# One input load moved from SyncE's queue to GpSimd's, and five filler matmuls fewer, at the start of an attention-plus-MLP kernel

## The chip, the cores and the metric

The kernel runs on one core of a Trainium2 chip. The metric is the device time of one execution in microseconds (us); for the kernel before it is the median of six runs. Five engines work side by side, each through its own list of instructions in order: TensorE (PE, matrix products), VectorE (DVE), ScalarE (ACT), GpSimd (POOL) and SyncE (SP, which here only issues DMAs). DMAs are issued from the lists of SP and GpSimd (one tiny one from ACT) and are carried out by 16 DMA engines; an engine that needs the data waits on a semaphore until the whole transfer has landed.

## The reference

Four batches, eight heads, 768 positions, head dimension 64. A linear attention with a decay `lam` per head is followed by a two-layer MLP with a gated activation. All inputs and the output are float32.

```
for each block b of 64 positions:
    intra = ((q_b k_b^T) * Dmask) v_b          # Dmask[i, j] = lam^(i-j) for i >= j, else 0
    inter = (q_b * lam^(i+1)) kv_state
    out_b = intra + inter
    kv_state = lam^64 * kv_state + (k_b * lam^(63-j))^T v_b
x = out, heads side by side                     # 3072 tokens x 512
h = x @ w_in                                    # 512 -> 2048
y = (h * sigmoid(1.702 h)) @ w_out              # 2048 -> 512
```

## The kernel before

The 768 positions are cut into waves. Waves 0 and 1 (`ND = 2`) each take two of the four batches with 256 positions of each; the four later waves take 128 positions of all four batches. So each wave gives 512 tokens to the MLP. A wave's attention is done while TensorE still works on the MLP of the wave before; only wave 0 has nothing ahead of it. The order of the instructions is written out by hand (`tc.manual_schedule()`, L457): wave 0 line by line (L458 to L512), then a list of MLP steps (`main`) into which attention steps (`side`) are put at given places (L545 to L577). The engines carry out their lists in just that order.

**Loads.** `load(0)` (L104) issues k, q, v of batch 0 and then k, q, v of batch 1 of wave 0 through SP, each 512 KB, most of them in two halves of four heads; v of batch 1 is one transfer. Each contiguous piece is 512 bytes. The weights are float32 in memory and bf16 in SBUF, so they are loaded by DMAs that convert, from GpSimd's list: `load_w_in(0)` to `(4)` (L175, tiles of 256, 256, 512, 512, 512 columns) and `load_w_out(0)` to `(3)` (L180). `gate_pool` (L451) makes GpSimd wait for the first half of v of batch 0 before it issues the first weights. `gate_sync` (L454, used at L506) makes SP wait until `w_out1` has landed; only then does SP issue `load(1)`, the inputs of wave 1.

**Attention of wave 0.** `do_cast` (L189) multiplies k or q by powers of `lam` and writes bf16: on VectorE for batch 0 and for q of batch 1, on GpSimd for k of batch 1 (L480). `turn_pe` (L228) transposes the result on TensorE and copies it out of PSUM with VectorE or ScalarE. `cast_v` (L219) converts v to bf16; of batch 1, one half on ScalarE and one on GpSimd (L499). `d_scores` (L247) makes the scores, VectorE masks them (L263); `split=True` lets ScalarE copy half of the scores out of PSUM first (L261). `d_one`/`d_state` (L280, L269) make the state from k and v, `d_out` (L304) the output from scores and v.

**The MLP.** `mlp1` (L387) and, for wave 0's first columns, `mlp1_half` (L397) compute the first layer from the `w_in` tiles; `mlp2` (L411) the second from `w_out`. In wave 0 the halves use `w_in0` and `w_in1`; the first full step of L393 is the first to use `w_in2`.

**Order around the change.** GpSimd's list at this place: gate on v of batch 0, `load_w_in(0)`, four multiplications of k of batch 1 (L198), `load_w_in(1)`, `load_w_in(2)`, its half of v of batch 1 (L211), `load_w_in(3)`, `(4)`, `load_w_out(0)` to `(3)`. TensorE's list: `fill(n)` (L139) puts n matmuls on a zero tile in front of or between the first transposes and scores; their result is never read. On TensorE, `mlp1_half(0, 0, 0)` (L509) stands ahead of `d_one(0, 1)` (L510), the first matmuls to read v of batch 1. On ScalarE, the half of v of batch 1 stands between the two copies of batch 1's scores.

Of the kernel before, what the change touches and what calls it, by code (L numbers as in the profile page):

```python
# [24 lines left out]
def kernel(  # L25
# [13 lines left out]
    nc = tc.nc  # L39
# [36 lines left out]
    def load_one(w, c, nm, src):  # L76
        x = ld.tile([P, H, 2 * D], f32, tag=f"{nm}{c}", name=f"{nm}f")
        if w < ND:
            n = H if w or (nm == "v" and c) else H // 2
            for h in range(0, H, n):  # L80
                nc.sync.dma_start(  # L81
                    out=x[:, h : h + n],
                    in_=src[2 * w + c, h : h + n, 0 : 2 * P, :].rearrange("h (s a) d -> s h (a d)", a=2))
        else:
            nc.sync.dma_start(out=x.rearrange("p h (a d) -> p (h a) d", a=2),
                              in_=src[2 * c : 2 * c + 2, :, w * P : (w + 1) * P, :].rearrange("b h s d -> s (b h) d"))
        loaded[w, c, nm] = x

    def load(w, nms="kqv"):
        src = {"k": k, "q": q, "v": v}  # L90
        if w < ND:
            for c in range(HF):
                for nm in nms:
                    load_one(w, c, nm, src[nm])
        else:
            for nm in nms:
                for c in range(HF):
                    load_one(w, c, nm, src[nm])
# [3 lines left out]
    ones = const.tile([1, P], f32)  # L102
    nc.vector.memset(ones, 1.0)
    load(0)  # L104

    nc.scalar.preload_act_table_set("natural_log_exp_and_others")
# [29 lines left out]
    def acc(name, dt=f32, shape=None, tag="a"):  # L136
        return ps.tile(shape or [P, 4, P], dt, tag=tag, bufs={"a": 5, "mm": 3}[tag], name=name)

    def fill(n, new=None):  # L139
        if new:  # L140
            fill_ps[0] = acc("ps_fill", shape=[P, W], tag=new)
        for _ in range(n):
            nc.tensor.matmul(fill_ps[0], zero[:, 0:P], zero, start=True, stop=True)  # L143
# [31 lines left out]
    def load_w_in(j):  # L175
        c0 = sum(IN_CH[:j]) * P
        nc.gpsimd.dma_start(  # L177
            out=w_in_sb[j], in_=moe_w_in.rearrange("(kc ki) f -> ki kc f", ki=P)[:, :, c0 : c0 + IN_CH[j] * P])
# [10 lines left out]
    def do_cast(w, c, nm, eng, g=None):  # L189
        if g in (None, 0):  # L190
            cast[w, c, nm] = work.tile([P, 2, HD], bf16, tag=f"{nm}s{c}", name=f"{nm}s")
        f, x = loaded[w, c, nm], cast[w, c, nm]
        if w < ND:
            pw = {"k": kd_pow, "q": qd_pow}[nm]
            for R in (0, 1) if g is None else (g,):
                for j in range(2):
                    h = slice(4 * R + 2 * j, 4 * R + 2 * j + 2)
                    eng.tensor_tensor(x.rearrange("p a (r i j d) -> p r j i a d", i=2, j=2, d=D)[:, R, j],  # L198
                                      f[:, h].rearrange("p i (a d) -> p i a d", a=2),
                                      pw[:, h].unsqueeze(3).to_broadcast([P, 2, 2, D]), op=MUL)  # L200
        else:
            pw = {"k": k_pow, "q": q_pow}[nm]
            n = 2 * H // 4
            for j in range(2):
                eng.tensor_tensor(x.rearrange("p b (r i j d) -> p j (b r) i d", i=2, j=2, d=D)[:, j],  # L205
                                  f.rearrange("p h (a d) -> p (h a) d", a=2).rearrange("p (n j i) d -> p j n i d", j=2, i=2)[:, j],
                                  pw.rearrange("p b (r j i) -> p j (b r) i", i=2, j=2)[:, j].unsqueeze(3).to_broadcast([P, n, 2, D]),
                                  op=MUL)
# [19 lines left out]
    def turn_pe(w, c, nm, copy=act_copy, g=None):  # L228
        x = cast[w, c, nm]
        rr = list(range(NP)) if g is None else [2 * g, 2 * g + 1]  # L230
        t = acc("ps_t", bf16, [P, len(rr), 2, P])
        for i, r in enumerate(rr):
            for a in range(2):
                nc.tensor.transpose(t[:, i, a, :], x[:, a, r * P : (r + 1) * P], ident)  # L234
        if g in (None, 0):
            trans[w, c, nm] = work.tile([P, 2 * NP, P], bf16, tag=f"{nm}T{c}", name=f"{nm}T")
        copy(trans[w, c, nm][:, 2 * rr[0] : 2 * rr[0] + 2 * len(rr)], t.rearrange("p r a s -> p (r a) s"))
# [9 lines left out]
    def d_scores(w, c, pp, split=False):  # L247
        kT = trans[w, c, "k"]
        s2 = [acc("ps_s") for _ in range(2)]
        for i in range(2):  # L250
            r = 2 * pp + i
            for a in range(2):
                for blk, bs in enumerate((A, Z)):
                    for h, hs in enumerate((A, Z)):
                        nc.tensor.matmul(s2[h][bs, 2 * i + a, :], kT[hs, 2 * r + a, bs], q_of(w, c, hs, r, blk),  # L255
                                         start=True, stop=True)
        for h in range(2):
            sm = work.tile([P, 2, 2, P], bf16, tag="sm", bufs=8, name="sm")
            flat = s2[h].rearrange("p (i a) s -> p i (a s)", i=2)
            if split and h:  # L260
                nc.scalar.copy(sm.rearrange("p i a s -> p i (a s)"), flat)  # L261
                flat = sm.rearrange("p i a s -> p i (a s)")
            nc.vector.tensor_tensor(sm.rearrange("p i a s -> p i (a s)"), flat,  # L263
                                    mask_d.rearrange("p o a b s -> p o (a b s)").to_broadcast([P, 2, 2 * P]), op=MUL)
            masked[w, c, pp, h] = sm
# [185 lines left out]
    def gate_pool(x):  # L451
        nc.gpsimd.tensor_copy(behind_q, x)
# [4 lines left out]
    with tc.manual_schedule():  # L457
# [4 lines left out]
            nc.scalar.activation(blk_pow[rows].rearrange("p (r i) -> p r i", i=2),  # L462
                                 ln_lam[rows].rearrange("p (r j i) -> p r j i", i=2, j=2)[:, :, j, :], EXP, scale=1.0 * P)
        nc.scalar.activation(warm, q_pow[:, 0, 0:1], GELU)
        fill(5)
        for nm, copies in (("k", (dve_copy, act_copy)), ("q", (act_copy, dve_copy))):
            for g in range(2):
                do_cast(0, 0, nm, nc.vector, g)
            for g in range(2):
                turn_pe(0, 0, nm, copies[g], g)  # L470
                fill(2 if nm == "k" or g == 0 else 0)
        gate_pool(loaded[0, 0, "v"][0:1, 0, 0:1])
        load_w_in(0)
        cast_v(0, 0, (act_copy, act_copy))
        d_scores(0, 0, 0)
        fill(1)
        d_scores(0, 0, 1)
        fill(3)
        for g in range(2):
            do_cast(0, 1, "k", nc.gpsimd, g)  # L480
        for j in (1, 2):
            load_w_in(j)
        d_one(0, 0, "mm")
# [18 lines left out]
        for j in range(NCH):  # L502
            load_w_out(j)
        nc.gpsimd.affine_select(mask, mask, pattern=[[0, 1], [1, P]], channel_multiplier=-1, base=0,
                                compare_op=mybir.AluOpType.is_ge, fill=0.0)
        gate_sync(w_out_sb[1][0:1, 0, 0:2])  # L506
        load(1)
        d_scores(0, 1, 1, True)
        mlp1_half(0, 0, 0)  # L509
# [36 lines left out]
        for w in range(NW):  # L546
            n = len(main)
            main += mlp_items(w)
            e = len(main)
            x = w + 1  # L550
            if x < ND:
                for c, (k_at, q_at, v_at, k_turn, q_turn, s_at, e_at) in enumerate(
                        ((19, 20, 19, 24, 25.5, 27, 30), (26.5, 28, 28, 29, 30, 32, 34))):
                    side += [(n + k_at, (do_cast, x, c, "k", (nc.vector, nc.gpsimd)[c])),
                             (n + q_at, (do_cast, x, c, "q", nc.vector)),
                             (n + v_at, (cast_v, x, c, ((pool_copy, pool_copy), (act_copy, act_copy))[c])),
                             (n + k_turn, (turn_pe, x, c, "k", act_copy)),
                             (n + q_turn, (turn_pe, x, c, "q", act_copy)),
                             (n + s_at, (start, x, c)), (n + e_at, (end, x, c))]
            elif x < NW:  # L560
                for c in range(HF):
                    tk, tq = (n + 2.1 + 2 * c, n + 4 + c) if x == ND else (n + 4 + 2 * c, n + 5 + 2 * c)
                    side += [(tk, (do_cast, x, c, "k", nc.vector)), (tk, (turn_dma, x, c, "k")),
                             (tq, (do_cast, x, c, "q", nc.vector)), (tq, (turn_dma, x, c, "q")),
                             (n + 10 + 2 * c, (cast_v, x, c, (dve_copy,)))]
                if x == ND:
                    side += [(n + 7, (stores,))]
                t = n + 16
                side += [(t, (n_two, x, 0)), (t + 4, (n_two, x, 1)), (t + 9, (n_rest, x))]
            if w + 2 < NW:  # L570
                side += [(n + (12 if w else 20), (load, w + 2))]
# [36 lines left out]
```

## Time and profile before

| What | Value |
|---|---|
| median of six runs | 208.05 us (207.48 to 208.66) |
| the profiled execution, its own time | 208.51 us |
| the profiled execution, span from first to last instruction | 206.8 us |
| TensorE busy | 201.3 us, 97% of the span |
| VectorE, ScalarE, GpSimd busy | 89.2, 86.1, 16.2 us |
| HBM read, written | 27.26 MB, 6.29 MB |
| filler matmuls (L143) | 20, 8.0 us busy, 518 ns mean |

The span is what the profile's clock runs over; the execution's own time holds 1.7 us more around it. Times in the profile count from the start of the span. A row such as `7.92 0.95 POOL L177 ...` gives start, duration, engine and line; what stands in square brackets is how long the engine had been idle and what released it. A queue marked POOLq or SPq belongs to the engine that issues the DMA. TensorE's busy share says little here: matmuls are pipelined, and fillers count as busy.

### The profile page before, as it was taken

The numbers are of one execution on the slowest core, as the hardware profiler recorded it, in microseconds if no ns is written. First come the engines' busy times: TensorE is split into PE (matmuls) and PEld (weight loads), VectorE is DVE, ScalarE is ACT, GpSimd is POOL, SyncE is SP. The second block draws the span as 40 slices with busy tenths as digits, with TensorE's granted clock in tenths as the row PEclk, the third lists the DMA queues.
The fourth block names the chain that finished last, engine by engine and source line by source line (L and its number), as shares of the span: only waits on it lengthen the run. The fifth ranks groups of instructions, "written<-read, shape, count | busy, mean of one in ns | idle before, by whom it ended". The sixth has DMA issues, their size and how long they took to land.

```text
span 206.8 us, 4295 instructions
## 1 busy us (share of the span) xinstructions
PE 201.3 (97%) x1830; PEld 105.1 (51%) x1830; DVE 89.2 (43%) x160; ACT 86.1 (42%) x158; POOL 16.2 (8%) x37
## 2 busy tenths in 40 slices
PE   7999899999999999999999999999999999999994
PEld 2576344466864464444464444464444454444453
DVE  1793000586961843931743841743841731100121
ACT  4877562147665030566021566021466021565000
POOL 4496000060000000000000000000000000000000
DMA  5999999999997999879971379961360011100112
GB/s 155 335 226 185 201 204 242 270 310 240 249 221 169 214 264 247 200 177 251 236 206 51 103 179 267 222 199 52 101 155 0 36 68 51 51 0 0 54 51 101
DMA packets 87640, 33.82 MB, mean 164 GB/s; under 512 B 67398, under 2 KB 84678, under 8 KB 87622
## 3 DMA queue, kind: packets, MB, share of 16 engines
q1 hardware_dynamic: 82868, 29.37, 56.3%
q0 software_dynamic: 4752, 4.19, 12.9%
q8 instruction: 14, 0.23, 0.5%
q14 instruction: 4, 0.03, 0.1%
q10 hardware_dynamic: 2, 0.00, 0.0%
HBM read 27.26 MB, written 6.29 MB: 162 GB/s over the span
## 4 chain that ended last, share of the span: by engine, by line
PE 88%; DMA 7%; SPq 1%; POOL 1%; issue 0%; DVE 0%; POOLq 0%
PE ps_out L417 41%; PE ps_h L393 35%; DMA w_in<-in_moe_w_in_dram 4%; PE ps_h L405 3%; DMA kf<-in_k_dram 2%; PE ps_s L331 2%; PE ps_o L381 2%; SPq L81 1%; POOL ks L198 1%; PE ps_o L368 1%; PE ps_t L234 1%; PE ps_kv L355 1%; PE ps_o L312 1%; PE ps_s L255 1%; PE ps_kv L275 0%; POOL w_in L177 0%
## 5 line engine op out<-in xcount | busy, mean ns | idle before, releaser
L417 PE MATMUL ps_out<-w_out,g_sb 128*128 128x512 bf16 (+2 forms) x416 | 86.2, 363 | 0.0
L393 PE MATMUL ps_h<-xT,w_in 128*128 128x512 bf16 x336 | 73.5, 379 | 0.8 <-DMA w_in<-in_moe_w_in_dram 0.8
L395 ACT ACTIVATE g_sb<-ps_h 128x512 bf16<-128x512 f32 x84 | 50.2, 597 | 46.1 <-PE ps_h L393 46.1
L417 PEld LDWEIGHTS <-g_sb 128*128 128x128 bf16 x416 | 38.2, 98 | 41.0
L393 PEld LDWEIGHTS <-w_in 128*128 128x128 bf16 x336 | 32.8, 98 | 40.3 <-DMA w_in<-in_moe_w_in_dram 1.1
L421 DVE COPY o_sb<-ps_out 128x512 f32<-128x512 f32 (+2 forms) x26 | 16.9, 650 | 52.4 <-PE ps_out L417 52.4
L339 DVE SCALAR_TENSOR_TENSOR sm<-ps_s,inv_pow,mask 128x512 bf16<-128x512 f32 x32 | 21.8, 742 | 28.5 <-PE ps_s L331 22.3
L385 ACT CAST xT<-ps_o 128x512 bf16<-128x512 f32 x16 | 8.2, 599 | 37.8 <-PE ps_o L381 37.8
L198 DVE TENSOR_TENSOR ks<-kf,kd_pow 128x256 bf16<-128x256 f32 x8 | 2.9, 420 | 22.9 <-DMA kf<-in_k_dram 19.6
L405 PE MATMUL ps_h<-xT,w_in 128*128 128x256 bf16 x96 | 11.4, 273 | 0.0
L205 DVE TENSOR_TENSOR qs<-qf,q_pow 128x512 bf16<-128x512 f32 x16 | 10.3, 683 | 0.0
L205 DVE TENSOR_TENSOR ks<-kf,k_pow 128x512 bf16<-128x512 f32 x16 | 10.3, 683 | 0.0
L405 PEld LDWEIGHTS <-w_in 128*128 128x128 bf16 x96 | 9.0, 98 | 1.6 <-DVE xT L214 0.2
L143 PE MATMUL ps_fill<-zero 128*128 128x512 bf16 x20 | 8.0, 518 | 1.4 <-DVE zero L113 1.4
L263 DVE TENSOR_TENSOR sm<-ps_s,mask_d 128x512 bf16<-128x512 f32 x14 | 8.8, 684 | 0.8 <-PE ps_s L255 0.5
L407 ACT ACTIVATE g_sb<-ps_h 128x512 bf16<-128x512 f32 x12 | 7.2, 598 | 4.3 <-PE ps_h L405 4.3
L359 DVE SCALAR_TENSOR_TENSOR kv<-kv,blk_pow,ps_kv 128x256 bf16<-128x256 bf16 x12 | 5.0, 475 | 6.0 <-PE ps_kv L355 6.0
L217 ACT COPY kT<-ps_t 128x512 bf16<-128x512 bf16 (+1 forms) x4 | 3.2, 797 | 8.1 <-PE ps_t L234 8.1
L198 DVE TENSOR_TENSOR qs<-qf,qd_pow 128x256 bf16<-128x256 f32 x16 | 5.7, 417 | 0.1
L331 PEld LDWEIGHTS <-kT 64*128 64x128 bf16 x128 | 3.6, 94 | 3.4 <-issue 3.4
L214 DVE CAST v_sb<-vf 128x1024 bf16<-128x1024 f32 x8 | 5.1, 683 | 0.0
L331 PE MATMUL ps_s<-qT,kT 64*128 64x128 bf16 x128 | 5.0, 217 | 0.0
(68 smaller groups left out, 91.4 us busy)
## 6 DMA issues: line engine op xcount, KB each, us to landing
vf<-in_v_dram SPq DMA_DIRECT2D x11, 512.0 KB, 6.4
kf<-in_k_dram SPq DMA_DIRECT2D x10, 512.0 KB, 5.8
qf<-in_q_dram SPq DMA_DIRECT2D x10, 512.0 KB, 6.5
out_dram<-o_sb SPq DMA_DIRECT2D x15, 256.0 KB, 2.0
out_dram<-o_sb SPq DMA_DIRECT2D x17, 128.0 KB, 2.4
w_out<-in_moe_w_out_dram POOLq DMA_DIRECT2D x4, 512.0 KB, 16.2
w_in<-in_moe_w_in_dram POOLq DMA_DIRECT2D x3, 512.0 KB, 9.8
kf<-in_k_dram SPq DMA_DIRECT2D x4, 256.0 KB, 3.1
```

The source lines that it names most:

```text
L143: nc.tensor.matmul(fill_ps[0], zero[:, 0:P], zero, start=True, stop=True)
L198: eng.tensor_tensor(x.rearrange("p a (r i j d) -> p r j i a d", i=2, j=2, d=D)[:, R, j], f[:, h].rearrange("p i (a d) -> p i a d", a=2), p ...
L205: eng.tensor_tensor(x.rearrange("p b (r i j d) -> p j (b r) i d", i=2, j=2, d=D)[:, j], f.rearrange("p h (a d) -> p (h a) d", a=2).rearran ...
L263: nc.vector.tensor_tensor(sm.rearrange("p i a s -> p i (a s)"), flat, mask_d.rearrange("p o a b s -> p o (a b s)").to_broadcast([P, 2, 2 * ...
L331: nc.tensor.matmul(s2[h][:, b, :], kT[hs, (b % 2) * NP + p, :], qT[hs, (b % 2) * NP + p, :], start=True, stop=True)
L339: nc.vector.scalar_tensor_tensor(sm, s, inv_pow[:, n : n + 1], mask.to_broadcast([P, B, P]), op0=MUL, op1=MUL)
L385: nc.scalar.copy(xT[w][:, p, :], ps_o.rearrange("p b s -> p (b s)"))
L393: nc.tensor.matmul(h, w_in_sb[j][:, kc, i * P : (i + 1) * P], xT[w][:, kc, :], start=(kc == 0), stop=(kc == KC - 1))
L395: nc.scalar.activation(g_of[w][:, fc, :], h, GELU)
L405: nc.tensor.matmul(h[:, u, :], w_in_sb[j][:, kc, i * P : (i + 1) * P], xT[w][:, kc, cols], start=(kc == 0), stop=(kc == KC - 1))
L417: nc.tensor.matmul(ps_out, g_of[w][:, fc, g * P : (g + 1) * P], w_out_sb[j][:, fc % CW, c0:c1], start=(fc == 0), stop=(fc == FFC - 1))
L421: nc.vector.tensor_copy(o, ps_out)
```

## The change

Two things are done. First, v of batch 1 of wave 0 is left out of `load(0)` and is issued from GpSimd's list after the four multiplications of k of batch 1 and ahead of `load_w_in(1)`. The transfer is the same one: 512 KB, float32 on both sides, into the same tile. Second, the fillers become fewer: 3 in place of 5 after the powers, then 2, 1, 1, 0 in place of 2, 2, 2, 0 behind batch 0's four transposes, and none in place of 1 between its two groups of scores. The four at the very start, the three after the scores and the one further on stay. One line is added at L94, so in the kernel after every later line has a number higher by one, but for those between the filler taken out at L476 and the added load (L477 to L480), which keep theirs.

```diff
         if w < ND:
             n = H if w or (nm == "v" and c) else H // 2
             for h in range(0, H, n):
-                nc.sync.dma_start(
+                (nc.gpsimd if w == 0 and c and nm == "v" else nc.sync).dma_start(
                     out=x[:, h : h + n],
                     in_=src[2 * w + c, h : h + n, 0 : 2 * P, :].rearrange("h (s a) d -> s h (a d)", a=2))
...
             for c in range(HF):
                 for nm in nms:
-                    load_one(w, c, nm, src[nm])
+                    if w or c == 0 or nm != "v":
+                        load_one(w, c, nm, src[nm])
...
         nc.scalar.activation(warm, q_pow[:, 0, 0:1], GELU)
-        fill(5)
+        fill(3)
         for nm, copies in (("k", (dve_copy, act_copy)), ("q", (act_copy, dve_copy))):
             for g in range(2):
                 do_cast(0, 0, nm, nc.vector, g)
             for g in range(2):
                 turn_pe(0, 0, nm, copies[g], g)
-                fill(2 if nm == "k" or g == 0 else 0)
+                fill(2 - g if nm == "k" else 1 - g)
         gate_pool(loaded[0, 0, "v"][0:1, 0, 0:1])
         load_w_in(0)
         cast_v(0, 0, (act_copy, act_copy))
         d_scores(0, 0, 0)
-        fill(1)
         d_scores(0, 0, 1)
         fill(3)
         for g in range(2):
             do_cast(0, 1, "k", nc.gpsimd, g)
+        load_one(0, 1, "v", v)
         for j in (1, 2):
             load_w_in(j)
```

## The prediction, made before the result was known

> **What bounds the kernel now.** I read the chain that ended last first. From 21.40 us on it is TensorE without a gap to the end, so all that counts is when that dense stretch starts and whether it is interrupted. Columns: start us, duration us, what.
>
> ```profile
> 9.35 2.33 POOL ks L198 x4
> 11.68 0.75 POOL w_in L177
> 12.43 8.92 DMA w_in<-in_moe_w_in_dram
> 21.35 0.05 issue
> 21.40 10.53 PE ps_h L393 x48
> ```
>
> The dense stretch starts when `w_in2` has landed, at 21.35. The timeline of the first 22 us shows the work around it.
>
> ```profile
> 7.92 0.95 POOL L177 DMA_DIRECT2D w_in<-in_moe_w_in_dram  x1
> ...
> 11.63 1.55 POOL L177 DMA_DIRECT2D w_in<-in_moe_w_in_dram  x2
> ...
> 13.50 0.61 POOL L211 CAST v_sb<-vf 128x512 bf16<-128x512 f32 x1 [0.32 <-DMA vf<-in_v_dram]
> ...
> 14.73 1.05 PE L405 MATMUL ps_h<-xT,w_in 128*128 128x256 bf16 x8
> ...
> 14.99 0.62 ACT L217 CAST v_sb<-vf 128x512 bf16<-128x512 f32 x1
> ...
> 15.71 0.37 PE L275 MATMUL ps_kv<-v_sb,ks 64*64 64x64 bf16 x12
> ...
> 21.40 0.82 PE L393 MATMUL ps_h<-xT,w_in 128*128 128x512 bf16 x3 [0.81 <-DMA w_in<-in_moe_w_in_dram]
> ```
>
> TensorE was done with all before L393 at 21.40 - 0.81 = 20.59 and stood still 0.81 us for `w_in2`. v of batch 1 landed at 13.48 (7.88 issue + 5.6 to landing, by the issues), 1.5 us before ScalarE got to its half at 14.99; TensorE's L275 at 15.71 follows on that half (done 15.61). Then the DMA by window, three windows: 10.0 to 10.5, 12.5 to 13.0, 20.0 to 21.4 us. Columns: queue, packets, MB, share of 16 engines' time.
>
> ```profile
> q1 hardware_dynamic: 336, 0.17, 113.2%
> ```
> ```profile
> q0 software_dynamic: 159, 0.08, 118.6%
> q1 hardware_dynamic: 49, 0.02, 21.8%
> ```
> ```profile
> q0 software_dynamic: 280, 0.27, 119.1%
> q8 instruction: 1, 0.02, 4.3%
> ```
>
> The 16 engines are full throughout (shares over 100% are overlapping packets), first with SP's loads, then with GpSimd's. The weights were issued at 7.92, yet between 8 and 12 us only 25 software packets start against 2617 hardware ones: GpSimd's transfers run when SP's are through. In the third window one instruction fetch of 4.3% x 16 x 1.4 us = 0.96 us sits on a DMA engine just before `w_in2` lands. Last, the timeline of wave 1's first transposes:
>
> ```profile
> 38.18 1.43 DVE L198 TENSOR_TENSOR ks<-kf,kd_pow 128x256 bf16<-128x256 f32 x4 [19.56 <-DMA kf<-in_k_dram]
> 39.54 0.61 PE L234 MATMUL ps_t<-ident,ks 128*128 128x128 bf16 x8
> ```
>
> VectorE waits 19.56 us for k of wave 1, which lands at about 38.16; its four products end at 39.61, and the second four transposes, which read the later two, run from about 39.54 + 4 x 0.056 = 39.76. So this landing has about 0.1 us of slack. It too hangs on the DMA queue: SP issues it only when `w_out1`, seventh in GpSimd's line of weights, has landed. The start of the kernel is bound by the DMA in two places, at 21.4 and at 39.6.
>
> [...] fillers start 0.42 us apart until 7.4 us and 0.22 us after.
>
> **The change part by part.**
>
> *Fillers.* Removed are two ahead of 5.83, at 0.42 us each, one behind the second and one behind the third transpose (0.2 to 0.4 us each), one at 9.37 (0.22). What waits on the first two: the first transposes start at 5.83, while VectorE's first products were ready at 5.35 + 0.1; so 0.4 us is won. VectorE's kT copy follows (6.50 becomes 6.1, as its products end at 6.06), and everything of batch 0 moves with it: scores 9.02 to about 8.5, masks 9.55 to 9.05, `d_out` and batch 1's q likewise. GpSimd's k of batch 1 does not move, it starts on a landing (9.35), but the transposes on it have room (first pair ready 10.5). The one at 9.37 costs nothing today: the second scores at 9.69 wait on the qT copy, 9.04 + 0.42. Sum: TensorE reaches L405 at 14.2 in place of 14.73. Unknown is the clock: [...] turns, scores and three fillers take about 0.4 + 0.7 + 0.6 us more at half speed, partly beside VectorE's masks. Bounds 0 to 0.6 us lost; I take 0.
>
> *SP's queue without v.* 512 KB in 512-byte packets are 1024 packets. The hardware queue moves 336 in 0.5 us, so its end comes 1024/672 = 1.5 us earlier, at 10.0 to 11.5 by engine in place of 11.5 to 13.0. `w_in0` (512 packets, 32 per engine, at 47 ns apiece: 85 per 0.25 us between 13.25 and 14.5) is then through at 11.5 to 13.0 and lands at about 13 in place of 14.5 (7.92 + 6.6). L405, moved to 14.2, so finds its weights; with `w_in0` at 14.5 it would not have.
>
> *v on GpSimd's queue.* It can be issued only after the four products of k, at 11.65. One issue of L177 takes 0.75 us, with half as many packets; so 0.75 to 1.5 us. [...] Data: 64 packets per engine at 24 ns (the hardware queue's rate, low end) to 47 ns (`w_in0`'s, which read 1 KB each, high end), 1.5 to 3.0 us; I take 28 ns, from the line through 47 ns for 1 KB and 82 ns for 2 KB read (855 packets in 4.4 us), 1.8 us. With 0.4 us to land: 14.8 to 15.3 on undisturbed engines; on the one that fetches instructions (0.96 us at 14.04, then inside this transfer) up to 16.2. Bounds 14.5 to 16.5, taken 15.8.
>
> *Who waits for that.* ScalarE would reach its half at 14.5 and stands until 15.8; behind it are the second copy of scores, the GELU of L405, both state copies, xT. TensorE stands at L275, GpSimd at L211. The whole tail from 14.99 to 20.59 moves by 15.8 - 14.99 = 0.8 us: TensorE is ready for L393 at 21.4. The 0.5 us of the fillers and the 0.81 us of idle time are both eaten; alone this gives no change. Behind L211 in GpSimd's list stand `w_in3` to `w_out3`: issued from about 16.4 in place of 14.05, while the line still has `w_in2` to move until 18 or later; no gap.
>
> *The DMA line.* Bytes are the same, so nothing is gained. Two things are lost. Between `w_in0` (through at 11.5 to 13.0) and v (12.6 to 13.1) the engines stand idle: 0 to 1.6 us, for the later engines, which set landings, about 0.5. And 64 x (28 - 24) ns = 0.26 us, since the software queue is slower per packet. Sum 0.8 us (bounds 0 and 1.9). All that follows, `w_in2` and k of wave 1 included, lands that much later: `w_in2` at 22.1, k at 38.9. SP's added wait is none; it loses an issue.
>
> *Sum.* The first bound gives 22.1 against 21.35, +0.75; the second 0.8 less 0.1 of slack, +0.7. They are one delay, not two. The profiled execution, 208.51 (span 206.8, 1.7 around it), would become 209.2; against the median of 208.05, which is 0.46 lower, 208.8.
>
> **The rivals.**
>
> *The early half microsecond arrives (faster).* Deciding place: the one DMA engine that carries the instruction fetch at 20.18, with `w_in2`'s last packets behind it. [...] if it falls behind `w_in2`, that lands up to 0.96 us earlier, at about 20.4. With v landed by 15.0, TensorE is ready at 20.6: gain 0.8 us, 207.3, if k of wave 1 lands by 37.4 as well. The point from which it decides is v at 15.0 together with no idle DMA. For it: 0.81 us stand open at L393. Against it: the second bound has 0.1 us slack and its bytes are unchanged.
>
> *All is hidden (no change).* v starts right behind `w_in0` (the late engines are through only at 13.0), and the delay is 0.26 us or less: 208.1.
>
> *v itself is the bound (slower by more).* Issue 1.5 us, packets at 47 ns, the fetch inside: v at 16.8, TensorE ready at 22.4, +1.0; with half the clock's loss 209.3. For it: nothing in the trace shows a cold start of GpSimd's queue. Against it: w_in issues take 0.75 us whatever their size.
>
> That the change doesn't do what it says is excluded by GpSimd's list, where v stands behind the products and ahead of `w_in1`.
>
> **How the numbers follow.** About 0.3%, 0.6 us, is what a measurement of this kernel can tell from no change. Main case 0.45 (208.8, own range 208.4 to 209.2; a fifth of it lies within 0.3%), larger delay 0.19, no change 0.14, faster 0.22. Faster by over 0.3%: 0.20; within: 0.02 + 0.14 + 0.09 = 0.25; slower: 0.36 + 0.19 = 0.55. The range from 207.5 to 209.7 leaves out most of the faster case's better half and the worst of the larger delay, about 0.2 together.
>
> **What would show it.** Right: scores near 8.5; L405 at 14.2; v landing near 15.8, with ScalarE idle for it ahead of L217; few packets around 12 to 13 us; L393 starting at about 22.1 on `w_in2`; VectorE's wait for k of wave 1 ending near 38.9. Wrong, if L393 starts before 21.4, if v lands before 15.0, if the DMA share has no dent at 12 to 13, or if k of wave 1 lands before 38.2.

## The result, and the profile after

The changed kernel takes 210.15 us in the median (33 executions, 209.10 to 211.64), the kernel before 208.45 (70 executions, 207.02 to 210.64). The ratio is 1.008, with a 95% interval of 1.0063 to 1.0098: slower by about 1.7 us. Forecast were 0.75 us and, against the first six runs, 208.8; the range ended at 209.7. The profiled execution of the changed kernel took 209.43 us (span 207.7), so it is one of the shorter ones; a second profile (below) shows one that took 210.94. That of the kernel before took 208.51.

The chain that ended last, of the changed kernel (start, duration, what). Before the change it ran from the weights' issue to `w_in2` and then over TensorE alone.

```profile
9.44 2.28 POOL ks L199 x4
11.71 4.53 DMA vf<-in_v_dram
16.30 0.61 POOL v_sb L212
16.91 1.44 POOL w_in L178 x2
18.35 0.71 POOL w_out L182
19.06 13.36 DMA w_out<-in_moe_w_out_dram
...
33.26 5.83 DMA kf<-in_k_dram
39.11 1.44 DVE ks L199 x4
```

The moved load is now in the chain, behind GpSimd's products, and from there the chain runs through GpSimd's weights and k of wave 1 to 39.11 (before: 38.18). TensorE takes over only there. Its timeline with that of ScalarE and GpSimd, changed kernel:

```profile
14.46 1.05 PE L406 MATMUL ps_h<-xT,w_in 128*128 128x256 bf16 x8
...
16.27 0.62 ACT L218 CAST v_sb<-vf 128x512 bf16<-128x512 f32 x1 [1.45 <-DMA vf<-in_v_dram]
16.30 0.61 POOL L212 CAST v_sb<-vf 128x512 bf16<-128x512 f32 x1 [2.13 <-DMA vf<-in_v_dram]
...
16.94 0.38 PE L276 MATMUL ps_kv<-v_sb,ks 64*64 64x64 bf16 x13 [1.43 <-ACT v_sb L218]
...
21.70 2.54 PE L394 MATMUL ps_h<-xT,w_in 128*128 128x512 bf16 x11
```

L406 is earlier by 0.27 us (before: L405 at 14.73), then three engines wait for v, and L394 begins at 21.70 in place of 21.40. No wait for `w_in2` is left: TensorE itself is late. At wave 1 it meets the second delay, a late k:

```profile
39.11 1.43 DVE L199 TENSOR_TENSOR ks<-kf,kd_pow 128x256 bf16<-128x256 f32 x4 [19.22 <-DMA kf<-in_k_dram]
...
39.93 0.40 PE L235 MATMUL ps_t<-ident,ks 128*128 128x128 bf16 x4
40.60 0.40 PE L235 MATMUL ps_t<-ident,ks 128*128 128x128 bf16 x4 [0.27 <-DVE ks L199]
```

Where the DMA time went, first before and then after: three stretches of 1 us, the last three columns being granted clock, DMA share and GB/s.

```profile
12.00:13.00 1.00, 0.94 (x38) 0.87 (x34) 1.00 (x5) 0.64 (x3) 1.00 (x2) 1.00 1.35 228
13.00:14.00 1.00, 1.00 (x15) 0.55 (x12) 0.81 (x4) 0.85 (x3) 0.68 (x2) 1.00 1.31 170
14.00:15.00 1.00, 1.00 (x36) 0.80 (x36) 0.85 (x2) 0.91 (x3) 1.00 (x3) 1.00 1.30 173
```
```profile
12.00:13.00 1.00, 1.00 (x38) 0.85 (x32) 1.00 (x4) 0.65 (x2) 1.00 (x2) 1.00 0.34 45
13.00:14.00 1.00, 1.00 (x26) 0.65 (x26) 0.80 (x3) 0.93 (x2) 1.00 (x2) 1.00 0.70 74
14.00:15.00 1.00, 1.00 (x33) 0.79 (x22) 0.85 (x3) 0.73 (x2) 0.17 (x1) 1.00 0.79 254
```

The shares sum to 1.83 in place of 3.96; at the 1.32 or so that these three stretches show before, an estimate is that 2.1 / 1.32 = 1.6 us of the DMA line are empty. That is the hole that the prediction named; it is larger.

### The profile page after: what moved, and what is told of

Its sections match the earlier page's. It is cut to its first block, busy times and chain, and to the rows that moved or that the text cites. A ratio compares the mean times of both kernels' runs of the same rounds, so it can differ in the third digit from the quotient of the medians.

```text
span 207.7 us, 4286 instructions
## 1 busy us (share of the span) xinstructions
PE 200.4 (96%) x1825; PEld 104.6 (50%) x1825; DVE 89.3 (43%) x160; ACT 86.3 (42%) x158; POOL 17.0 (8%) x38
## 4 chain that ended last, share of the span: by engine, by line
PE 79%; DMA 14%; POOL 2%; SPq 2%; DVE 1%; issue 0%; POOLq 0%
PE ps_out L418 37%; PE ps_h L394 30%; DMA w_out<-in_moe_w_out_dram 6%; DMA kf<-in_k_dram 5%; PE ps_h L406 3%; DMA vf<-in_v_dram 2%; PE ps_s L332 2%; PE ps_o L382 2%; SPq L81 1%; PE ps_o L369 1%; POOL ks L199 1%; PE ps_t L235 1%; PE ps_kv L356 1%; DVE ks L199 1%; POOL w_in L178 1%; PE ps_o L313 1%
## 5 line engine op out<-in xcount | busy, mean ns | idle before, releaser
L394 PE MATMUL ps_h<-xT,w_in 128*128 128x512 bf16 x336 | 73.5, 379 | 0.0
L418 PEld LDWEIGHTS <-g_sb 128*128 128x128 bf16 x416 | 38.2, 98 | 41.0
L394 PEld LDWEIGHTS <-w_in 128*128 128x128 bf16 x336 | 32.9, 98 | 39.2
L406 PE MATMUL ps_h<-xT,w_in 128*128 128x256 bf16 x96 | 11.4, 273 | 0.0
L406 PEld LDWEIGHTS <-w_in 128*128 128x128 bf16 x96 | 9.0, 98 | 1.7 <-DVE xT L215 0.2
L144 PE MATMUL ps_fill<-zero 128*128 128x512 bf16 x15 | 6.6, 546 | 1.4 <-DVE zero L114 1.4
```

The source lines that it names most:

```text
L394: nc.tensor.matmul(h, w_in_sb[j][:, kc, i * P : (i + 1) * P], xT[w][:, kc, :], start=(kc == 0), stop=(kc == KC - 1))
L406: nc.tensor.matmul(h[:, u, :], w_in_sb[j][:, kc, i * P : (i + 1) * P], xT[w][:, kc, cols], start=(kc == 0), stop=(kc == KC - 1))
L418: nc.tensor.matmul(ps_out, g_of[w][:, fc, g * P : (g + 1) * P], w_out_sb[j][:, fc % CW, c0:c1], start=(fc == 0), stop=(fc == FFC - 1))
```

## The experiments

Theory H: the hole in the DMA line makes all that follows on it late, `w_in2` and the loads of wave 1. Theory V: the wait for v itself is the cost. Theory F: the missing fillers cost clock. Theory C came up after the second profile: the wait for v costs clock.

### e1_changed_again: the changed kernel once more

> The changed kernel once more, for a second profile. Theory H (hole): the cost is DMA time left empty between the first weights and v on GpSimd's queue, which delays w_in2 and k of wave 1; so k of wave 1 lands about 1 to 1.7 us later than in the kernel before (38.2), VectorE's wait for it ends near 39 to 40, and the ratio is 1.004 to 1.010. Theory V (late v): the cost is the wait of ScalarE, GpSimd and TensorE for v itself (v landed at 16.25 in the first profile); then TensorE's start of L394 (21.70 there) holds the loss, and nothing later adds to it. Theory F (fillers): the loss comes from the clock; then the transposes and scores before 10 us are slower than in the kernel before.

Ratio 1.0088 (1.0058 to 1.0119). This profile (210.94 us) shows what the first one didn't. Timeline of TensorE:

```profile
17.45 0.38 PE L276 MATMUL ps_kv<-v_sb,ks 64*64 64x64 bf16 x13 [1.45 <-ACT v_sb L218]
...
19.63 4.32 PE L406 MATMUL ps_h<-xT,w_in 128*128 128x256 bf16 x24
23.78 1.46 PE L394 MATMUL ps_h<-xT,w_in 128*128 128x512 bf16 x6
```

The same 24 matmuls took 2.84 us in the first profile. The half clock lasted from 19.37 to 22.79 us. TensorE's busy time and, third from the end, its granted clock in stretches of that length, laid so that the half clock fills one of them, second profile:

```profile
12.55:15.96 3.41, 3.38 (x77) 1.00 0.67 157
15.96:19.37 3.41, 1.73 (x72) 1.00 1.22 185
19.37:22.79 3.42, 3.42 (x19) 0.50 1.09 156
```

TensorE was busy for 1.73 of 3.41 us in the stretch with the wait, and the next stretch ran at half clock. In the first profile, which has no half clock to lay the stretches by, one of that length with the wait is this, and the clock stayed:

```profile
14.64:18.05 3.41, 1.81 (x56) 1.00 1.14 224
```

The mean granted clock of every execution is known, so they can be told apart. Of 50 of the changed kernel (34 with the first profile among them, and 16 here), 22 have a mean clock of 0.992 or less, with a median of 210.50 us; the other 28 have a median of 209.56. Of 58 executions of the kernel before, measured beside these 16, 6 were at such a clock; the other 52 have a median of 208.18. So at full clock the change costs about 1.4 us, and the 44% of its executions with a half clock took 0.9 more. k of wave 1: VectorE's products start at 39.40.

### e2_fillers_only and e3_v_only: the two halves of the change

```diff
-        fill(5)
+        fill(3)
...
-                fill(2 if nm == "k" or g == 0 else 0)
+                fill(2 - g if nm == "k" else 1 - g)
...
-        fill(1)
```

> v stays on SyncE's queue, only the five fillers go. H and V: no loss, ratio 0.997 to 1.003, since w_in2 (21.35) and k of wave 1 (38.2) land as before and the 0.3 to 0.5 us won ahead of them are waited away at L393. F: most of the loss is here, ratio 1.004 or more.

Ratio 1.0014 (0.9983 to 1.0044); none of 14 executions at half clock. The fillers are not the cause: F falls. This profile (209.23 us, 0.9 above the run's median) also shows how far landings move from one execution to the next, with v where it was:

```profile
15.57 1.05 PE L405 MATMUL ps_h<-xT,w_in 128*128 128x256 bf16 x8 [0.87 <-DMA w_in<-in_moe_w_in_dram]
...
39.00 1.43 DVE L198 TENSOR_TENSOR ks<-kf,kd_pow 128x256 bf16<-128x256 f32 x4 [19.36 <-DMA kf<-in_k_dram]
```

k of wave 1 is here nearly as late as in the changed kernel, against the expectation of 38.2, and the time is that of the changed kernel at full clock. One pair of profiles therefore can't carry a difference of 0.9 us; the medians do.

```diff
-                nc.sync.dma_start(
+                (nc.gpsimd if w == 0 and c and nm == "v" else nc.sync).dma_start(
...
+        load_one(0, 1, "v", v)
         for j in (1, 2):
             load_w_in(j)
```

> v goes to GpSimd's queue, the fillers stay as before. H and V: the whole loss, ratio 1.006 to 1.010. V expects it to be a little larger than in the changed kernel only if v's landing is later; H expects the same hole of about 1.5 us. F: no loss, ratio about 1.000.

Ratio 1.0084 (1.0057 to 1.011): all of the loss. 7 of 19 executions at a lower clock; in the profiled one TensorE waited 2.24 us for v and then ran two stretches at half clock (18.39 to 25.21 us; 0.984 in the mean).

### e4_v_early: v ahead of GpSimd's products

```diff
         load_w_in(0)
+        load_one(0, 1, "v", v)
...
-        load_one(0, 1, "v", v)
```

> As the changed kernel, but v is issued right behind w_in0, ahead of the four products of k on GpSimd, so that the queue never runs empty. H: no hole; w_in2 and k of wave 1 land within 0.3 us of the kernel before (21.35 and 38.2), v lands near 14.5, ratio 0.996 to 1.002. V: v is early too, so the same ratio; this run does not tell H from V, but both fall if the loss stays at 1.005 or more, and a price per packet of GpSimd's queue (0.26 us in the prediction) would be left as the cause.

Ratio 1.0024 (1.0002 to 1.0046), just above the expected range, and none of 22 executions at half clock. v landed at 14.7, L394 started at 20.82, VectorE's products of wave 1 at 37.96. So the order behind the products, not GpSimd's queue as such, makes nearly all of the loss. As the expectation says, this does not tell H from V, for the hole and the lateness of v go together. What is left, half a microsecond with an interval that nearly reaches nothing, was not explained. Later the line was not full here either (shares 0.70, 0.85 and 0.75 in the microseconds from 15, 16 and 18), and k was not late: empty time on the line does not turn into a late landing one for one.

### e5_w_in1_first: the hole filled, v still late

```diff
         load_w_in(0)
+        load_w_in(1)
...
-        for j in (1, 2):
+        for j in (2,):
```

> As the changed kernel, but w_in1 is issued ahead of the four products of k on GpSimd, so that the queue has work while v is waited for; v itself stays where it is and, with one more transfer ahead of it, lands at 15.8 to 16.8. Theory H (the hole in the DMA line delays w_in2 and k of wave 1): no hole, k of wave 1 lands near 38.2, ratio 1.000 to 1.004. Theory C (TensorE stands 1.4 us or more for v at L276, [...] and in some executions runs at half clock for one or two windows of 3.4 us): the wait stays, so the loss stays, ratio 1.005 to 1.011, with single times up to 211 and more.

Ratio 1.0109 (1.0058 to 1.0159). The line stayed full where the hole had been (share 1.35 and 1.22 from 12 to 14 us), but v landed at 17.3, later than expected, TensorE waited 2.04 us, and 4 of 6 executions are at a lower clock (median 211.65; the two others 209.27 and 209.94). H's ratio is missed. Nor did the line stay full: GpSimd, which stands at its half of v, issues `w_in3` and all behind it only then.

```profile
17.32 0.61 POOL L212 CAST v_sb<-vf 128x512 bf16<-128x512 f32 x1 [3.43 <-DMA vf<-in_v_dram]
17.87 1.48 POOL L178 DMA_DIRECT2D w_in<-in_moe_w_in_dram  x2
```

From 18 to 20 us the share is 0.70 and 0.79, with 114 and 43 GB/s. So the run moves the hole and makes v later; it does not take the hole away. What it does give back is the landing of `w_out1`: SP goes on at 31.57, as before the change (31.53; changed 32.44). k's products begin at 38.87 all the same, because its transfer takes 6.5 us from its issue in place of 5.8. The profiled execution, in stretches of the same length:

```profile
15.14:18.55 3.41, 1.37 (x48) 1.00 1.14 247
18.55:21.96 3.41, 3.29 (x52) 0.50 0.89 114
21.96:25.38 3.42, 3.42 (x18) 0.50 1.24 205
```

### e6_hole_only and e12_hole_clean: the hole, v early

```diff
+        for _ in range(3):
+            nc.gpsimd.tensor_copy(spare2, spare)
         for j in (1, 2):
             load_w_in(j)
```

> The kernel before, v on SyncE's queue and all fillers, with three copies of a spare tile on GpSimd (1.8 us, work that is added) ahead of w_in1's issue: a hole in the DMA line, but v lands early, near 13.5. H: w_in2 and k of wave 1 land 0.7 to 1.7 us later, ratio 1.003 to 1.008. C: TensorE doesn't wait for v, no half clock, so no more than what the DMA line loses where TensorE is not ahead of it; if C is the whole cause the ratio is 0.998 to 1.003.

Ratio 1.0114 (1.0076 to 1.0152). (The making of the two spare tiles is left out above.) `w_in2` landed at about 23.0 and wave 1's products began at 39.90, each 1.7 us later. But the test is not clean: beside the copies VectorE's products of q took 0.82 us each in place of 0.42, TensorE waited 1.3 us for them, and 3 of 6 executions are at half clock, the profiled one among them:

```profile
11.70:15.11 3.41, 1.95 (x52) 1.00 0.81 141
15.11:18.52 3.41, 3.41 (x75) 0.50 0.99 133
```

Hence a second run, in which GpSimd only waits (the tile `behind_p` is made further up):

```diff
-        for j in (1, 2):
-            load_w_in(j)
...
         do_cast(0, 1, "q", nc.vector, 1)
+        nc.gpsimd.tensor_copy(behind_p, cast[0, 1, "q"][0:1, 1, HD - 1 : HD])
+        for j in (1, 2):
+            load_w_in(j)
```

> The kernel before, v on SyncE's queue and all fillers; w_in1 and w_in2 are issued by GpSimd only after VectorE's last product of q of batch 1 (about 13.4 us in place of 11.65), by a one-element copy that waits for it. So the DMA line has a hole between w_in0 (through at about 13.7) and w_in1 (first packets about 15), and no engine gets other work, which e6_hole_only couldn't keep (its copies slowed VectorE's products from 0.42 to 0.82 us). H: w_in2 and k of wave 1 land 1 to 1.7 us later than in the kernel before (21.35 and 38.2), ratio 1.004 to 1.009, with no execution at half clock. If the hole costs nothing by itself: ratio 0.998 to 1.002.

Ratio 1.0191 (1.0144 to 1.0239), 5 of 6 executions at full clock: more than was expected. Timeline, TensorE at the first full step of the MLP and VectorE at wave 1:

```profile
23.30 1.90 PE L394 MATMUL ps_h<-xT,w_in 128*128 128x512 bf16 x8 [1.98 <-DMA w_in<-in_moe_w_in_dram]
...
40.40 1.43 DVE L199 TENSOR_TENSOR ks<-kf,kd_pow 128x256 bf16<-128x256 f32 x4 [21.06 <-DMA kf<-in_k_dram]
```

`w_in2` is 1.9 us late, k of wave 1 2.2 us, in wave 2 the transposed q is late as well (TensorE waits 1.04 us for it at 69.72), and the span is 4.0 us longer. So weights that GpSimd issues late cost more than the change does, with v early and the clock full. This is what H says in kind, but not a copy of the hole in the changed kernel: there `w_in2` landed on time, and here GpSimd's wait also puts off the issue of `w_in3` and all behind it, from 14.05 to 16.34, and the line thins a second time (share 0.79 from 20 to 21 us). Why it costs 4 us and not 2 was not followed further.

### e7_fill_wait: TensorE kept busy while v is late

```diff
         mlp1_half(0, 0, 0)
+        fill(6, "mm")
         d_one(0, 1)
```

> The changed kernel with six fillers (1.3 us, results unread) between L510's mlp1_half and d_one(0, 1), so that TensorE is busy while it waits for v; nothing lands earlier. C: the clock stays whole and the executions with a half clock go; the ratio falls from 1.008 to 1.003 to 1.005, and the highest times fall below 210.5. H: nothing changes, ratio 1.006 to 1.010, for the DMA line is the same.

None of 16 executions is at half clock, against 22 of 50: C is confirmed in what it says of the clock. The median is 209.54, that of the changed kernel's executions at full clock (209.56), while the ratio, 1.0081 (1.0053 to 1.0109), is not below the changed kernel's beyond its interval. The expected 1.003 to 1.005 is missed, and so are the highest times (two of 211.60 and 211.87, at full clock): most of the loss is there at full clock. L394 starts at 22.17 in place of 21.40. VectorE's products of wave 1 start at 39.37, so TensorE waits for k:

```profile
40.30 0.39 PE L235 MATMUL ps_t<-ident,ks 128*128 128x128 bf16 x4
40.86 0.40 PE L235 MATMUL ps_t<-ident,ks 128*128 128x128 bf16 x4 [0.17 <-DVE ks L199]
```

### e8, e9, e10, e11: can k of wave 1 be had earlier?

e8 is e4_v_early with k released by `w_out0`:

```diff
-        gate_sync(w_out_sb[1][0:1, 0, 0:2])
-        load(1)
+        gate_sync(w_out_sb[0][0:1, 0, 0:2])
+        load_one(1, 0, "k", k)
+        gate_sync(w_out_sb[1][0:1, 0, 0:2])
+        for c, nm in ((0, "q"), (0, "v"), (1, "k"), (1, "q"), (1, "v")):
+            load_one(1, c, nm, {"k": k, "q": q, "v": v}[nm])
```

> v issued right behind w_in0 as in e4_v_early, and k of batch 0 of wave 1 released by w_out0 in place of w_out1, the other five loads of wave 1 by w_out1 as before. If the landing of k of wave 1 (37.9 with e4_v_early) is what holds TensorE at its first transposes of wave 1, it lands near 36 and the ratio falls 0.002 to 0.003 under that of e4_v_early, to 0.997 to 1.001; if w_in2's landing is what holds all, the ratio is that of e4_v_early, 1.000 to 1.005.

Ratio 1.0034 (1.0013 to 1.0055). Released 3 us earlier, k still landed at about 38.4: its transfer took 9.8 us in place of 6.1 (e4_v_early), side by side with the weights. The earlier release moved nothing here, so the run does not say what an earlier k would give.

e9, e10 and e11 are e4_v_early, the kernel before and e7_fill_wait with k of wave 1's batch 0 in two transfers:

```diff
-            n = H if w or (nm == "v" and c) else H // 2
+            n = H if (w and (c or nm != "k")) or (nm == "v" and c) else H // 2
```

> e4_v_early, with k of batch 0 of wave 1 loaded in two transfers of four heads each in place of one, so that VectorE's first two products don't wait for the whole. In the profiles so far the time of an execution at full clock is the start of VectorE's products of wave 1 plus 170.3 us (before 38.18 and 208.51, the changed kernel 39.11 and 209.43, e6_hole_only 39.90 and 210.18). If that landing is the bound, up to 0.7 us goes, two products of 0.36 us, until w_in2 or another load is late instead: ratio 0.996 to 1.000, and below that of e4_v_early (1.0024). If the relation is chance, the ratio stays at 1.001 to 1.004.

> The kernel before with the same two transfers. TensorE started L393 at 21.40 and came to wave 1's transposes about when k was ready, so where w_in2 sets the start nothing is won, and where k is late up to 0.7 us: ratio 0.996 to 1.000.

> e7_fill_wait (the changed kernel kept at full clock) with the same two transfers. If what was left of the loss there (209.5 against 208.1 us) is the late landing of k of wave 1, 0.4 to 0.7 us of it goes: ratio 1.003 to 1.006, and TensorE's start of L394 (22.2 there) becomes the bound. If the loss came from the wait for v alone, the ratio stays at 1.007 to 1.009.

Ratios 1.0031 (0.9999 to 1.0063), 0.998 (0.995 to 1.001) and 1.0069 (1.0039 to 1.0099). None of the three separates from its parent; e9 and e11 miss the ranges that were expected if k's landing is the bound. In e11 VectorE begins at 39.35, but q's products wait another 0.79 us and GpSimd's of batch 1 0.92 us (start 45.27): it is not one transfer that is late, but all of wave 1's loads. That the time is the start of VectorE's products plus 170.2 to 170.3 us holds in the profiles of the kernel before, of the changed kernel, of e2, e4, e7 and e8, and of e6, which was not at full clock (0.992 in the mean). It does not hold in e9 to e12 (170.8 to 172.1), nor in e1, e3 and e5 with their half clock (171.5 to 173.7). No version beat the kernel before clearly.

## Why the prediction was wrong

**The direction was right, and one of the two places.** The loss is in the moved load; the fillers alone change nothing measurable (e2). v landed at 16.25 (predicted 15.8, bounds 14.5 to 16.5), TensorE stood 1.43 us at L276, L406 came at 14.46 (predicted 14.2), TensorE was ready for L394 at 21.70 (predicted 21.4), and wave 1's products began at 39.11 (predicted 38.9). The other place failed: `w_in2` landed at 21.41 (issue 13.4 + 8.0), not at 22.1, and no wait for it shows. In the kernel before an instruction fetch of 0.96 us lies on a DMA engine just ahead of that landing, from 20.18; in the changed kernel one of 1.9 us starts at 19.74. Why the landing didn't move was not shown.

**The step that was mis-sized: the hole.** The prediction put it at 0.5 us, since `w_in0` was through "at 11.5 to 13.0" and v's first packet would come at 12.6 to 13.1, and counted the late DMA engines only. That start was the author's estimate; the profile before shows no transfer from GpSimd that starts on an empty line. In the changed kernel the line is empty earlier and starts later. The first packet comes at 13.37, 1.66 us after the start of the issue at 11.71; in the stretch from 13 to 14 us (40 slices of 25 ns, busy tenths):

```profile
DMA  0000000000000009000909990999090000009003
...
DMA packets 18, 0.07 MB, mean 74 GB/s; under 512 B 0, under 2 KB 0, under 8 KB 18
...
q0 software_dynamic: 18, 0.07, 70.4%
```

and these 18 packets of 4 KB took 70.4% x 16 us / 18 = 0.63 us each. In e1 the first packet comes 1.66 us after the issue too (12.29 to 13.95; share 0.15 from 13 to 14 us). The empty time is 1.6 us by the estimate above, the upper bound that the prediction gave its hole. In place of the 0.7 us that the prediction had for k of wave 1, it is 0.9 us late in the first profile and 1.2 in e1 and e7, and the medians at full clock are 1.4 us apart.

**The step that was put at nothing: the clock of TensorE's wait.** The prediction counted the clock for the fillers, but took TensorE's stand at L275 as a delay alone. In four profiles a half clock follows a stand of TensorE: after stretches of 3.41 us with 1.18 (e3), 1.37 (e5), 1.73 (e1) and 1.95 us (e6) busy the next ran at half clock, in e3 and e5 the next two. After one of 1.81 us (first profile) it didn't, so busy time alone gives no limit here. In the second profile the half clock makes the 24 matmuls of L406 1.48 us longer. With fillers in the wait none of 16 executions had it (e7), without them 22 of 50; by subtraction it makes the 0.3 us by which the loss in the medians, 1.7 us, exceeds that at full clock.

**What luck did.** v's landing lies within its bounds on a wrong account of its packets: the prediction had 64 packets of 512 bytes per engine, and v went as 128 packets of 4 KB, 8 per engine in the mean, which started later. (The rate of 28 ns was also misread: the line through 47 and 82 ns gives 29.5.) So the 0.26 us that it charged for slower packets has no basis. That the two profiled executions differ by 0.92 us, near the 0.75 forecast, is luck as well: the one of the kernel before is 0.3 us above its median at full clock, that of the changed kernel 0.1 us below.

**What is shown of the loss at full clock, and what is open.** Two delays run side by side, and the later one counts. In the first profile TensorE is 0.30 us late at L394 and k of wave 1 0.93 us, and the time is 0.92 us longer; in e7 it is 0.77, 1.19 and 1.19. So k sets the time in both; TensorE's own lateness is smaller and lies beneath it. For the hole as the reason why k is late speaks the landing of `w_out1`, which releases it: SP goes on at 32.4 to 33.4 us in the seven profiles with a hole behind `w_in0` (changed kernel, e1, e3, e6, e7, e11, e12) and at 31.1 to 32.0 in five without (before, e2, e4, e5, e10); e9, at 32.4, is an exception. But no run has the hole and nothing else. A further path, which the prediction dismissed with "no gap", is GpSimd's wait for v: it puts off the issue of `w_in3` to `w_out3` to 16.86, and the line thins at 17 and 20 us (shares 0.94 and 0.99, before 1.15 and 1.24). No run tests it alone; in e5, where it is stronger, `w_out1` was on time and only k's own transfer took longer. How the 1.4 us divide among these stays open.

**The rival that made v itself the bound** came nearest in size (209.3), with v at 16.8 (measured 16.25, and 16.76 in e1), but its clock loss was that of the fillers.

## What to carry to other kernels

Before a transfer is put behind a computation, ask what its queue has to move until the transfer's first packet, here 1.66 us after the start of the issue. It ran dry for an estimated 1.6 us; the next load was not late for it, but one that landed at 39 us was. Ask too what the engines that wait for the transfer would have issued next. Price a stand of TensorE twice: as the delay, and as the clock afterwards; here a stand of 1.4 to 2.2 us was followed, in some executions, by 3.4 or 6.8 us at half clock. When several delays run side by side, an experiment that removes only one need not show a gain; and one that adds a delay has to be read to the end, for here each moved other issues as well.

## What the runs showed of the hardware that was not expected

- The moved load went as 4 KB packets from GpSimd's queue (changed kernel, 13 to 14 us: 18 packets, 0.07 MB), though its contiguous pieces are 512 bytes and SyncE's queue moved its loads as packets of about 512 bytes (before, 8 to 12 us: 2617 packets, 1.31 MB).
- Its first packet came 1.66 us after the start of the issue, in the first profile (11.71 to 13.37) and in e1 (12.29 to 13.95).
- While three float32 copies ran on GpSimd (0.77 us each), VectorE's products beside them took 0.82 us in place of 0.42 (e6).
- SyncE's and GpSimd's transfers do not always keep one order: from 8 to 12 us of the kernel before 2617 hardware packets started and 25 software ones, while from 31 to 37 us of e8 it was 1969 and 588, at 59% and 57% of the engines' time.
